# One stage's attention values, token mixing and u, woven two pieces of the channel mixing later

## The chip, the cores and the metric

The kernel runs on one core of a Trainium2 chip. The metric is the time of one execution on the device in microseconds (us); lower is better. A profile of one execution goes with it, which records when each engine ran each instruction. The engines are TensorE (PE in the profile, with its weight loads as PEld), VectorE (DVE), ScalarE (ACT), GpSimd (POOL) and SyncE (SP, which issues DMAs).

## What is computed

Eight batches of attention over pooled keys and values, followed by a token-mixing and a channel-mixing layer with a residual. Cut to what matters:

```python
# q, k, v: (8 batches, 8 heads, 576 tokens, 64); pool = 8
k_p = k.reshape(B, H, Sp, pool, D).mean(axis=3)
v_p = v.reshape(B, H, Sp, pool, D).mean(axis=3)
scores = scale * np.matmul(q, k_p.transpose(0, 1, 3, 2))
attn = softmax(scores)
x = np.matmul(attn, v_p)            # heads side by side: (8, 576, 512)

xt = x.transpose(0, 2, 1)
h = np.maximum(xt @ w_tok1, 0.0) @ w_tok2       # over the tokens
u = x + h.transpose(0, 2, 1)
h2 = np.maximum(u @ w_ch1, 0.0) @ w_ch2         # over the channels, 1536 wide
out = u + h2
```

## The kernel before

The batches are numbered from 0, so "the fourth batch" is batch 3. Of a batch's 576 tokens, 512 form its main part, as four interleaved sets of 128 (j = 0 to 3); the last 64 are its tail. Tails are joined in pairs, batches (0, 7), (1, 2), (3, 4) and (5, 6), so that a pair fills 128 partitions. Work on a pair's tail happens with one of its two batches.

The steps of a batch, with the lines that appear in the profile:

- Loads of k, q and v on GpSimd's DMA queue (L138, L142, L146), started by `load_gated`: a small copy (L984) on GpSimd waits until the last transposed weights of an earlier batch are there, and the loads, a pairing of k (L269) and the pooling of v by additions (L357 to L359) stand behind it on that engine.
- q is turned by a DMA on the SP queue (L693), k is pooled by matmuls (L282 or L291), the scores are a matmul (L390), VectorE subtracts the maximum (L396, L398), ScalarE takes the exponential (L406).
- The weights are turned by a DMA transpose on the SP queue (L412, for a tail L535) into pT. There are two of them for each of the units a (j = 0, 1) and c (j = 2, 3).
- The values, `do_AV`: pT is the stationary operand and pooled v the moving one (L468). VectorE divides by the sum (L472, L473) and writes x. A `do_AV` is called a value block here.
- Token mixing: `do_tails` (L608) and, in two halves, `do_AT` (L615); the first half is activated by ScalarE (L591) and the second by VectorE (L593). Then u for each j (`do_u`, L672 with the addition L673 on VectorE), which a DMA transpose on SP turns, two j at a time (`do_uT`, L684, into uTm).
- Channel mixing, `c_stream`: twelve `do_GT` of four matmuls over 512 columns (L1007, activated by ScalarE in L1009), then for each j three thirds of an output block (L1023, four matmuls each), an addition on VectorE (L1027) and a store on the SP queue (L1055). For the second batch of a pair the same follows for the tail. Each `do_GT` and each third carries the cost 864 and is called a piece here.

The order of instructions on every engine is the order in which the program emits them; no scheduler moves them. A loop over the batches b emits, in each turn, a main stream and a side stream. The main stream is the channel mixing of batch b. The side stream holds what comes next: the turn of q for batch b+2, the gated loads for batch b+3, the value blocks, token mixing and u of batch b+1 (`value_stream`, `mix_stream`), and the scores of batch b+2 (`score_stream`). Each step has a cost in units, and `weave` merges the two streams: it takes a side step when the side's share of its cost is not ahead of the main stream's share. The main stream's count starts at minus `delay`, so that this much of it goes ahead of the first side step, and `lead` takes that much off its length, so that the side stream ends earlier:

```python
tm, ts = max(main.total() - delay - lead, 1e-9), max(side.total(), 1e-9)
cm, cs = -delay, 0.0
...
take_side = im >= len(main.items) or (ia < len(side.items) and cs / ts <= cm / tm)
```

PSUM tiles come from six rotating buffers, pT tiles from six, uTm and q's turned tiles from two each. A step's DMAs are issued where the step is emitted, and a queue takes its DMAs in order.

Of the kernel before, what the change touches and what calls it, by code (L numbers as in the profile page):

```python
# [28 lines left out]
def weave(main, side, delay=0.0, lead=0.0):  # L29


    tm, ts = max(main.total() - delay - lead, 1e-9), max(side.total(), 1e-9)
    im = ia = 0
    cm, cs = -delay, 0.0
    while im < len(main.items) or ia < len(side.items):
        take_side = im >= len(main.items) or (ia < len(side.items) and cs / ts <= cm / tm)
        if take_side:
            c, fn = side.items[ia]
            ia += 1
            cs += c  # L40
        else:
            c, fn = main.items[im]
            im += 1
            cm += c
        fn()
# [3 lines left out]
def kernel(  # L49
# [17 lines left out]
    B, H, S, D = q.shape  # L67
# [864 lines left out]
    def score_stream(st, b):  # L932

        add = adder(st)
        a, c, t = parts[b]
        own = owned(b)
        add(SC, a.do_S, 0)
        add(SC, a.do_S, 1)
        add(0, a.do_E, 0)
        for bb in own[1:]:  # L940
            add(KP, pool_k, bb)
        add(SC, a.do_S, 2)
        add(0, a.do_E, 1)
        add(0, a.do_E, 2)
        add(0, a.do_PT, 0)
        add(0, a.do_PT, 1)
        if t:
            add(2 * SC, t.do_S)
        add(SC, c.do_S, 0)
        if t:  # L950
            add(0, t.do_E)
            add(0, t.do_PT)
        add(SC, c.do_S, 1)
        add(0, c.do_E, 0)
        add(SC, c.do_S, 2)
        add(0, c.do_E, 1)
        add(0, c.do_E, 2)
        add(0, c.do_PT, 0)
        add(0, c.do_PT, 1)

    def value_stream(st, b):

        add = adder(st)
        a, c, t = parts[b]
        if b + 1 < B:
            units(b + 1)
            add(0, qT_dma, b + 1)
        if b + 2 < B:
            add(0, load_gated, b + 2, lambda: c.pT[1][:, 0, 0:1])
        add(AV, a.do_AV, 0)  # L970
        add(AV, a.do_AV, 1)
        if t and len(t.bs) == 1:
            add(AV, t.do_AV)
        add(AV, c.do_AV, 0)
        if t and len(t.bs) > 1:
            add(AV, t.do_AV)
        add(AV, c.do_AV, 1)
        mix_stream(st, b, owned(b + 1)[:1] if b + 1 < B else ())
# [70 lines left out]
    def c_stream(b):  # L1049
        st = Stream()  # L1050
        g = group_of[b]

        def dst_main(j, cols, o_sb):
            q = nc.gpsimd if b == B - 2 and j == 0 else nc.sync if cols.start == 0 else nc.scalar
            q.dma_start(out=out[b, 0:MAIN, cols].rearrange("(p j) n -> p j n", j=NJ)[:, j, :], in_=o_sb)  # L1055

        def dst_tail(j, cols, o_sb):
            for s, bb in enumerate(groups[g]):
                nc.sync.dma_start(out=out[bb, MAIN:S, :], in_=o_sb[half[s], :])

        wide, chunk = channel_mix(lambda kk, t0, t1: uT_main[b][:, t0 // P:t1 // P, kk, :],
                                  lambda j: u_main[b][:, j, :], dst_main, MAIN, 0 if b else 3)
        blocks = [wide] + [chunk(j, 2 if b == B - 1 and j == NJ - 1 else 1) for j in range(NJ)]
        if slot_of[b] == 1:
            wide, chunk = channel_mix(lambda kk, t0, t1: uT_tail[g][:, kk, t0:t1], lambda j: u_tail[g], dst_tail, P)
            at = 3 if b == B - 1 else len(blocks)
            blocks[at:at] = [wide, chunk(0)]
        for block in blocks:
            st.items.extend(block)
        return st  # L1070
# [16 lines left out]
    with tc.manual_schedule(engines=engines):  # L1087
        side1 = begin()
        for b in range(B):
            side = Stream() if b else side1  # L1090
            if 0 < b < B - 1:
                value_stream(side, b + 1)
            if b + 2 < B:
                score_stream(side, b + 2)

            weave(c_stream(b), side, 1728.0 if b == 0 else 3456.0 if b == 1 else 1728.0, 3456.0 if b == B - 2 else 1728.0)


# [28 lines left out]
```

## Time and profile before

| | us |
|---|---|
| median of three runs | 281.32 |
| lowest and highest | 279.86, 281.5 |
| the profiled execution | 280.83 |
| its span, first to last instruction | 279.1 |

The granted clock of TensorE was 1.0 of full speed. In the lines below a row of a timeline has its start in us, its length in us, the engine, the line, and what it writes and reads; in brackets stands the idle time of the engine before it and who ended it. A row of the chain of waits has a start, a length and what the time went to. A list of waits gives the engine, line and tile, whom it waited for, the sum in us, the number of times and the longest. A row of the windows gives for a stretch its length, the busy time of PE, PEld, DVE, ACT and POOL, the granted clock, the DMA engines' share and GB/s. The stage of interest is the channel mixing of batch 2, from about 95 to 128 us.

### The profile page before, as it was taken

The numbers are of one execution on the slowest core, as the hardware profiler recorded it, in microseconds if no ns is written. First come the engines' busy times: TensorE is split into PE (matmuls) and PEld (weight loads), VectorE is DVE, ScalarE is ACT, GpSimd is POOL, SyncE is SP. The second block draws the span as 40 slices with busy tenths as digits, with TensorE's granted clock in tenths as the row PEclk, the third lists the DMA queues.
The fourth block names the chain that finished last, engine by engine and source line by source line (L and its number), as shares of the span: only waits on it lengthen the run. The fifth ranks groups of instructions, "written<-read, shape, count | busy, mean of one in ns | idle before, by whom it ended". The sixth has DMA issues, their size and how long they took to land.

```text
span 279.1 us, 5476 instructions
## 1 busy us (share of the span) xinstructions
PE 268.3 (96%) x2144; PEld 145.1 (52%) x2172; DVE 165.6 (59%) x381; ACT 121.9 (44%) x225; POOL 113.4 (41%) x162
## 2 busy tenths in 40 slices
PE   6789999999999999999999999999999999999994
PEld 4565856554545444475545454475544454554462
DVE  5597677778759853684579761785479452510112
ACT  8673688235533454035534452054623550036220
POOL 8748433697538957193449264820000000000000
PEclk9999999999999999999999999999999999999999
DMA  8999999996999999959998999759266701461013
GB/s 134 176 195 205 200 205 196 190 212 140 197 153 193 222 239 153 212 151 155 173 197 144 204 199 194 162 137 162 63 84 152 180 2 39 113 100 33 38 47 105
DMA packets 98969, 42.27 MB, mean 151 GB/s; under 512 B 68800, under 2 KB 94400, under 8 KB 98944
## 3 DMA queue, kind: packets, MB, share of 16 engines
q0 software_dynamic: 35616, 17.93, 49.1%
q1 hardware_dynamic: 63184, 23.93, 42.4%
q8 instruction: 17, 0.28, 0.4%
q10 hardware_dynamic: 144, 0.07, 0.1%
q14 instruction: 8, 0.07, 0.1%
HBM read 35.85 MB, written 9.44 MB: 162 GB/s over the span
## 4 chain that ended last, share of the span: by engine, by line
PE 84%; DMA 6%; DVE 5%; issue 1%; ACT 1%; POOL 1%; DVEq 0%; POOLq 0%
PE pa L1023 31%; PE pa L1007 30%; PE pa L672 3%; DMA pT<-prob_m 3%; PE pa L390 3%; PE pa L468 3%; DMA km<-in_k_dram 2%; PE pa L597 2%; PE pa L651 1%; DVE xm L473 1%; PE pa L615 1%; PE pt L615 1%; DVE mx L396 1%; PE pa L1039 1%; PE pt L374 1%
## 5 line engine op out<-in xcount | busy, mean ns | idle before, releaser
L1023 PE MATMUL pa<-wc,GT 128*128 128x512 bf16 (+2 forms) x427 | 102.4, 373 | 1.0 <-issue 0.2
L1009 ACT ACTIVATE GT<-pa 128x512 bf16<-128x512 f32 x105 | 62.2, 597 | 64.1 <-PE pa L1007 63.8
L1007 PE MATMUL pa<-uTm,wc 128*128 128x512 bf16 x372 | 89.3, 379 | 0.0
L1007 PEld LDWEIGHTS <-wc 128*128 128x128 bf16 x564 | 44.8, 98 | 37.1 <-issue 1.6
L1023 PEld LDWEIGHTS <-GT 128*128 128x128 bf16 x444 | 40.8, 98 | 41.5 <-issue 1.2
L406 ACT ACTIVATE prob_m<-sh 128x432 bf16<-128x432 f32 (+1 forms) x48 | 24.5, 522 | 55.2 <-DVE sh L398 55.1
L1027 DVE TENSOR_TENSOR o<-pa,um 128x512 f32<-128x512 f32 (+2 forms) x33 | 22.1, 670 | 26.4 <-PE pa L1023 26.3
L357 POOL TENSOR_TENSOR s<-vs 72x512 f32<-72x512 bf16 x24 | 27.6, 1150 | 15.7 <-DMA vs<-in_v_dram 14.2
L398 DVE TENSOR_TENSOR sh<-pa,mx 128x432 f32<-128x432 f32 (+1 forms) x48 | 26.8, 558 | 4.1
L396 DVE TENSOR_REDUCE mx<-pa 128x6 f32<-128x432 f32 (+1 forms) x48 | 26.4, 550 | 4.3 <-PE pa L390 4.1
L473 DVE TENSOR_TENSOR xm<-pa,den 128x256 bf16<-128x256 f32 x56 | 23.7, 424 | 1.9
L1055 POOL DMA_DIRECT2D out_dram<-o x1 | 0.6, 620 | 49.1 <-DVE o L1027 49.1
L472 DVE RECIPROCAL den<-pa 128x4 f32<-128x4 f32 x60 | 10.6, 176 | 16.8 <-PE pa L468 16.7
L673 DVE TENSOR_TENSOR um<-pa,xm 128x512 bf16<-128x512 f32 x24 | 16.1, 687 | 5.0 <-PE pa L672 3.7
L358 POOL TENSOR_TENSOR s<-s 72x256 f32<-72x256 f32 x24 | 17.3, 722 | 1.9
L390 PE MATMUL pa<-kbd,qT 128*128 128x144 bf16 x128 | 15.2, 226 | 0.9 <-ACT qT L378 0.7
L390 PEld LDWEIGHTS <-qT 128*128 128x128 bf16 x128 | 10.6, 98 | 9.3 <-ACT qT L378 1.3
L468 PEld LDWEIGHTS <-pT 72*128 72x128 bf16 (+1 forms) x256 | 11.2, 99 | 8.1 <-DMA pT<-prob_m 1.4
L593 DVE TENSOR_SCALAR AT<-pa 128x512 bf16<-128x512 f32 x6 | 4.1, 692 | 16.9 <-PE pa L615 9.5
L672 PE MATMUL pa<-AT,w2m 128*128 128x512 bf16 x45 | 13.1, 379 | 0.0
L468 PE MATMUL pa<-vpx,pT 72*128 72x65 bf16 (+1 forms) x256 | 12.6, 194 | 0.5 <-DMA pT<-prob_m 0.4
L1007 PE MATMUL pa<-uTt,wc 128*128 128x128 bf16 x192 | 11.9, 219 | 0.0
(151 smaller groups left out, 273.5 us busy)
## 6 DMA issues: line engine op xcount, KB each, us to landing
out_dram<-o SPq DMA_DIRECT2D x30, 256.0 KB, 2.6
vs<-in_v_dram POOLq DMA_DIRECT2D x7, 512.0 KB, 10.7
km<-in_k_dram POOLq DMA_DIRECT2D x7, 512.0 KB, 9.6
qm<-in_q_dram POOLq DMA_DIRECT2D x7, 512.0 KB, 12.8
wc<-in_moe_w_ch_dram POOLq DMA_DIRECT2D x6, 512.0 KB, 11.7
out_dram<-o SPq DMA_DIRECT2D x8, 128.0 KB, 2.4
o<-in_k_dram SPq DMA_DIRECT2D x2, 256.0 KB, 3.0
kt<-in_k_dram POOLq DMA_DIRECT2D x8, 64.0 KB, 8.0
```

Source lines behind the costliest of these rows:

```text
L357: nc.gpsimd.tensor_tensor(out=s4, in0=vs[:, hs, 0:4], in1=vs[:, hs, 4:8], op=add)
L390: nc.tensor.matmul(out=sc[:, (h - h0) * 2:(h - h0) * 2 + 2, :], lhsT=qTs[self.b][:, 2 * h + self.jj, :], rhs=kbd[self.b % NB][:, h], start ...
L396: nc.vector.tensor_reduce(out=mx[:, 0:n], in_=sc, axis=AX.X, op=ALU.max)
L398: nc.vector.tensor_tensor(out=sh[:, 0:n], in0=sc, in1=mx[:, 0:n, None].broadcast_to([P, n, SP]), op=ALU.subtract)
L406: nc.scalar.activation(out=self.probs[:, :, h0:h1, 0:SP].rearrange("p e h n -> p h e n"), in_=self.sh[i][:, 0:(h1 - h0) * 2].rearrange("p ...
L468: nc.tensor.matmul(out=ao[r, hh, :], lhsT=probs_of(h, r), rhs=vpx[b % NB][:, h, :], start=True, stop=True)
L473: nc.vector.tensor_tensor(out=xo[rows, hf * HP * D:(hf + 1) * HP * D].rearrange("p (h d) -> p h d", d=D), in0=ao[rows, :, 0:D], in1=den[ro ...
L672: nc.tensor.matmul(out=u_ps, lhsT=w2m[:, m, j, :], rhs=ATs[b][:, m, :], start=(m == 0), stop=(m == 1))
L1007: nc.tensor.matmul(out=g_ps[:, i, :], lhsT=wc1[:, kk, m * P:(m + 1) * P], rhs=uTs(kk, 0, width), start=(kk == 0), stop=(kk == 3))
L1009: nc.scalar.activation(out=GT[:, m0:m0 + per, :], in_=g_ps, func=AF.Relu)
L1023: nc.tensor.matmul(out=hold["ps"], lhsT=GT[:, kk, j * P:(j + 1) * P], rhs=wc2[:, kk, cols], start=(kk == 0), stop=(kk == NM - 1))
L1027: nc.vector.tensor_tensor(out=o_sb, in0=hold["ps"], in1=us(j)[:, cols], op=ALU.add)
```

## The change

One argument, the delay, in the loop over the batches. It was 1,728 units in the first turn, 3,456 in the turn of batch 1, and 1,728 afterwards. Now the turn of batch 2 has 3,456 as well. Nothing else is edited.

```diff
-            weave(c_stream(b), side, 1728.0 if b == 0 else 3456.0 if b == 1 else 1728.0, 3456.0 if b == B - 2 else 1728.0)
+            weave(c_stream(b), side, 1728.0 if b == 0 else 3456.0 if b <= 2 else 1728.0, 3456.0 if b == B - 2 else 1728.0)
```

In the turn of batch 2 the emitted order is, before and now (GT0 to GT11 and out0.0 to out3.2 are pieces, a and c the value blocks, t that of the tail pair, S the scores of batch 4, tGT and outT the tail's channel mixing):

```
before: GT0-1 | a.AV0 | GT2-3 | a.AV1 | GT4-5 | c.AV0 | GT6-7 | t.AV | GT8 | c.AV1 | GT9-10 | tails | GT11
        | AT.0 | out0.0 | AT.1 | out0.1-2 | u0 | out1.0 | u1 | out1.1 | uT0, u2 | out1.2 | u3 | out2.0
        | uT2, a.S0 | out2.1 | a.S1 | out2.2, out3.0 | a.S2 | out3.1-2 | c.S0 | tGT0 | c.S1 | tGT4-8 | c.S2 | outT
now:    GT0-3 | a.AV0 | GT4-5 | a.AV1 | GT6-7 | c.AV0 | GT8 | t.AV | GT9-10 | c.AV1 | GT11, out0.0 | tails
        | AT.0 | out0.1-2 | AT.1 | out1.0 | u0 | out1.1 | u1 | out1.2 | uT0, u2 | out2.0 | u3 | out2.1
        | uT2, a.S0 | out2.2 | a.S1 | out3.0-1 | a.S2 | out3.2 | c.S0 | tGT0-4 | c.S1 | tGT8 | c.S2 | outT
```

The turn of q for batch 4 and the gated loads of batch 5 are emitted just ahead of a.AV0 in both.

## The prediction

> **What bounds the kernel now.** I read the page first, then the waits, then the chain of waits in order of time around the fourth batch, then the timelines of the engines there. Batches are numbered from 0, so the fourth batch is batch 3. Its values, token mixing and u are woven into the channel mixing of batch 2.
>
> ```profile
> span 279.1 us, 5476 instructions
> PE 268.3 (96%) x2144; PEld 145.1 (52%) x2172; DVE 165.6 (59%) x381; ACT 121.9 (44%) x225; POOL 113.4 (41%) x162
> ```
>
> TensorE (PE) is busy in 96% of the span, and no other engine in more than 59%. A change of order that issues the same matmuls can therefore only gain the stretches in which PE stands, or make new ones. So the first question is which waits of PE the profile names in the place that the change touches.
>
> ```profile
> PEld L468 <- DMA pT<-prob_m: 1.4, 2, 0.9
> ...
> PE pa L468 <- DMA pT<-prob_m: 0.4, 1, 0.4
> ```
>
> In these lists of waits L468 is the matmul of the values, attention weights times pooled v. Its stationary operand is pT, the transposed weights, which a DMA on the SP queue writes. The weight loader waited for that DMA twice, 1.4 us in sum, and the matmul itself once for 0.4 us. The chain of waits says when.
>
> ```profile
> 91.01 6.13 DMA pT<-prob_m
> 97.15 0.04 issue
> 97.19 0.43 PE pa L468 x8
> 97.63 0.56 PE pa L1007 x3
> 98.18 3.21 DMA pT<-prob_m
> 101.39 0.05 issue
> 101.44 0.43 PE pa L468 x8
> ```
>
> Two of batch 3's transposes reach PE at the last moment: the first, issued at 91.01, lands at 97.14 and the matmuls begin at 97.19; the third, issued at 98.18, lands at 101.39 and its matmuls begin at 101.44. What PE does around them stands in its timeline:
>
> ```profile
> 94.94 1.89 PE L1007 MATMUL pa<-uTm,wc 128*128 128x512 bf16 x8
> 97.19 0.43 PE L468 MATMUL pa<-vpx,pT 72*128 72x65 bf16 x8 [0.36 <-DMA pT<-prob_m]
> 97.46 1.89 PE L1007 MATMUL pa<-uTm,wc 128*128 128x512 bf16 x8
> 99.19 0.42 PE L468 MATMUL pa<-vpx,pT 72*128 72x65 bf16 x8
> 99.45 1.89 PE L1007 MATMUL pa<-uTm,wc 128*128 128x512 bf16 x8
> 101.44 0.43 PE L468 MATMUL pa<-vpx,pT 72*128 72x65 bf16 x8
> 101.71 1.89 PE L1007 MATMUL pa<-uTm,wc 128*128 128x512 bf16 x8
> ```
>
> Each L1007 row holds two pieces of the channel mixing, four matmuls of 512 columns each. Where nothing waits, two pieces take 97.46 to 99.19, which is 1.73 us or 0.865 us a piece (0.216 us a matmul), and a value block takes 0.26 to 0.27 us (99.19 to 99.45). Against this spacing the first pair lasts from 94.94 to 97.19, 2.25 us, and so holds a wait of 0.52; the third lasts from 99.45 to 101.44, 1.99 us, a wait of 0.26. Together 0.78 us.
>
> **The change part by part.** In the weave the channel mixing starts from a negative count. With a delay of 1,728 units two pieces of 864 go ahead of the first side step; with 3,456 units four do. The side stream of this stage has 17,198 units, and the main stream 25,920, of which 25,920 - 1,728 - 1,728 = 22,464 were spread over before and 20,736 are now. So the side steps start two pieces later, run closer together and have caught up at the end. In the built order the value blocks come two pieces later, or nearly, token mixing, u and the scores of batch 4 about one piece later, and from the tail's channel mixing on one score block alone differs. Matmuls are neither added nor removed. The order on ScalarE is the same, and on GpSimd only buffer names differ.
>
> *The waits that go.* The first value block will begin at 94.94 + 4 x 0.865 = 98.40, with pT there since 97.14: 1.26 us to spare. The third block comes after eight pieces and two blocks, at 94.94 + 6.92 + 0.53 = 102.39, with its pT there since 101.39: 1.0 us to spare. When pT lands doesn't hang on the move, since the four transposes are issued between 91 and 101 from work that stands ahead of it. Both waits go: **minus 0.78 us**. From below this is bounded by the idle time that the windows show,
>
> ```profile
> 96.00:98.00 2.00, 1.64 (x15) 0.76 (x14) 1.34 (x4) 1.42 (x3) 1.84 (x3) 1.00 1.19 301
> ...
> 100.00:102.00 2.00, 1.90 (x17) 0.83 (x15) 0.86 (x5) 1.19 (x2) 0.00 (x0) 1.00 1.07 194
> ```
>
> where PE (second figure) lacks 0.36 and 0.10 us, 0.46 in sum, at a granted clock of 1.00; from above by the loader's 1.4 us. I take 0.78, since it is a distance between starts.
>
> The Trainium skill, "Perfetto Trace Analysis", section "Per-instruction lifecycle: what the profiler-reported window actually captures", says that the end of a TensorE instruction is estimated by the profiler and only the start is observed. By the modelled ends the gain would be 0.46 us, by the starts 0.78; the trace bears the page out, as the L1007 row of 1.89 us from 97.46 overlaps the value block that starts 1.73 us later.
>
> Another page speaks against the cover: "TensorE: Matmul & The Clock Gate" of the Trainium skill, section "Back-to-back issue gap", gives about 131 ns per matmul of 512 columns in a sustained stream. By that the four pieces would end at 94.94 + 16 x 0.131 = 97.04, 0.1 us before pT lands, and a little of the first wait would stay. The trace has 0.216 us, and goes.
>
> *Token mixing to u.* Before, two pieces stand between the second half of token mixing (L615) and u (L672); now one does, and VectorE has the first output block's addition (L1027) to do ahead of the activation instead of after it.
>
> ```profile
> 110.01 1.03 PE L615 MATMUL pa<-xm,w1m 128*128 128x512 bf16 x4
> 110.87 1.89 PE L1023 MATMUL pa<-wc,GT 128*128 128x512 bf16 x8
> 112.60 0.59 PE L672 MATMUL pa<-AT,w2m 128*128 128x512 bf16 x2
> ```
>
> ```profile
> 111.07 0.69 DVE L593 TENSOR_SCALAR AT<-pa 128x512 bf16<-128x512 f32 x1 [4.77 <-PE pa L615]
> ...
> 112.80 0.69 DVE L1027 TENSOR_TENSOR o<-pa,um 128x512 f32<-128x512 f32 x1 [1.03 <-PE pa L1023]
> ```
>
> Put in these times: the piece after token mixing starts at 110.87 and u at 110.87 + 0.865 = 111.74; u's first matmul reads the half that ScalarE wrote, the second, at 111.95, the half that VectorE finishes at 111.76. So 0.2 us to spare. The addition of 0.69 us becomes possible a token-mixing half (0.86 us) earlier and is over before. Cost: nothing; 0.5 us if the addition starts so late that all of its 0.69 us lies ahead of the activation.
>
> *SP's queue and batch 4.* Each side step takes its DMA along. qT of batch 4 keeps its place. The first turn of u goes behind the second output store, and the two turns follow each other; scores of batch 4 come one piece later, so the last ones' reduction on VectorE now stands ahead of the last output addition.
>
> ```profile
> 115.25 1.23 SPq L684 DMA_TRANSPOSE uTm<-um  x1
> 117.40 0.33 SPq L1055 DMA_DIRECT2D out_dram<-o  x1
> 118.00 1.28 SPq L684 DMA_TRANSPOSE uTm<-um  x1
> 121.34 2.51 SPq L1055 DMA_DIRECT2D out_dram<-o  x2
> 123.95 6.86 SPq L412 DMA_TRANSPOSE pT<-prob_m  x4
> ```
>
> The next rows are from the timelines of VectorE and PE; the last two are the landings of batch 4's pT and, over 84 to 140 us, of the turns of u.
>
> ```profile
> 121.78 0.46 DVE L398 TENSOR_TENSOR sh<-pa,mx 128x288 f32<-128x288 f32 x1
> ...
> 128.37 1.89 PE L1007 MATMUL pa<-uTm,wc 128*128 128x512 bf16 x8
> 130.09 0.42 PE L468 MATMUL pa<-vpx,pT 72*128 72x65 bf16 x8
> ...
> 134.33 0.42 PE L468 MATMUL pa<-vpx,pT 72*128 72x65 bf16 x8
> ...
> DMA to landing us min/median/max: 3.3/3.3/4.7
> ...
> DMA to landing us min/median/max: 3.0/4.0/9.5
> ```
>
> The second turn will be issued near 118 as now and is first read by the channel mixing of batch 3, which now starts at 128.37 - 0.78 = 127.6. Even after 9.5 us, the longest landing of a turn, it is there at 127.5. Nothing is added. Batch 4's four pT are issued back to back for 6.86 us, so a delay of the first is one of all: the last goes out near 123.95 + 6.86 - 1.3 = 129.5, lands 3.3 us later, at 132.8, and is read at 134.33. That is 1.5 us to spare. The last scores' reduction and subtraction (0.46 us in the row, and about as much for the reduction) now stand ahead of the last addition, and delay it, the last store and the transposes behind it by about 0.25 us against PE. Cost: nothing.
>
> *GpSimd.* Its order stays, and its next load waits for the fourth pT of batch 3, which doesn't move:
>
> ```profile
> 102.78 0.19 POOL L984 COPY gate<-pT 128x1 bf16<-128x1 bf16 x1 [3.14 <-DMA pT<-prob_m]
> ...
> 118.18 1.14 POOL L357 TENSOR_TENSOR s<-vs 72x512 f32<-72x512 bf16 x1 [5.74 <-DMA vs<-in_v_dram]
> ```
>
> The loads of batch 5 begin at 102.9 in both kernels, and PE wants nothing of them before the channel mixing of batch 3. Cost: nothing. Nor do PSUM's six rotating buffers bind: two are held through token mixing of batch 3, as before, and the others come free after a VectorE or ScalarE pass of 0.7 us or less (two for scores), four or more steps before they are wanted.
>
> The sum is -0.78 us. The profiled execution took 280.83 us (1.7 us around its span), so it would take 280.05. The three runs lie from 279.86 to 281.5 with the median at 281.32, 0.5 above the profiled one; the mean of the four is 280.88, which gives **280.1 us**.
>
> **The rivals.** *The gain is lost again later.* The loads of batch 5 keep their time while PE comes 0.78 us earlier, so that a wait could grow where PE meets them. Against it speaks that PE's list of waits names no other DMA that it waits for after the start of the kernel. The time: 280.8.
>
> *Batch 4's transposes come late.* The wait taken from batch 3 returns one stage on. Four pT stand in one row on SP behind two stores, and what PE has to spare at the last of them is 1.5 us. Should they land as slowly as batch 3's first, after 6.1 us instead of 3.3, they would be 2.8 + 0.25 late, a wait of 1.55 us, and the sum is 1.55 - 0.78 = 0.77 above now: 281.6. It decides from a delay of 1.5 us on, and is slower than now from 2.3. Against it: the run of four showed 4.7 us at most, and the loads of batch 5 have landed by 118.18, when GpSimd starts on the last of them.
>
> *The change doesn't remove the wait*, because PE waits for something else that becomes ready with pT. The values are the only other operand, and GpSimd ended its pass over them before these transposes were issued; the starts follow the landings by 0.05 us twice. It would give 280.8 as well, and goes with the first rival.
>
> **How the numbers follow.** The forecast gets 0.68, no gain 0.17, the late transposes 0.12; 0.03 is left for what I don't see. The range takes the upper bound of the gain, 280.83 - 1.4 = 279.4, the slower rival's 281.6, and some of the spread of the runs on both sides: 279.0 to 281.8. A per cent is 2.8 us, about what a measurement of this kernel can tell from no change; no case reaches it by itself. So within 1%: 0.89. Slower by more gets 0.07, for the slower rival where two batches pay it or the landing is that of 9.5 us; faster by more 0.04.
>
> **What would show it.** Right: in the new profile L468 no longer waits for pT, the four pieces from about 94.9 run at 0.86 us each, the first value block starts near 98.4 and the third near 102.4, and the channel mixing of batch 3 starts near 127.6 instead of 128.37. The AT step shows no PE wait ahead of L672. Wrong: an idle time of PE ahead of L672 near 112 us or of L468 near 130 to 134 us, or a start of batch 3's channel mixing at 128.3 or later.

## The result and the profile after

| | before | changed |
|---|---|---|
| median, 20 runs each (us) | 281.17 | 280.06 |
| lowest and highest | 279.61, 282.25 | 279.35, 281.59 |
| span of the profiled execution | 279.1 | 278.6 |

The ratio of the times is 0.9963 with a 95% interval of 0.9947 to 0.9978. On 281.17 us that is a gain of 1.04 us, between 0.62 and 1.49. The ratios in this document leave out runs more than 1.5% above the fastest run of the same kernel, which were one of `fill_after`'s twelve and four of `q_late`'s six.

First the page of the changed kernel, then PE's timeline around batch 3's values and at the end of the stage:

```profile
span 278.6 us, 5477 instructions
PE 267.4 (96%) x2144; PEld 145.0 (52%) x2172; DVE 165.8 (60%) x381; ACT 121.8 (44%) x225; POOL 113.8 (41%) x162
```

```profile
95.17 3.62 PE L1007 MATMUL pa<-uTm,wc 128*128 128x512 bf16 x16
98.63 0.42 PE L468 MATMUL pa<-vpx,pT 72*128 72x65 bf16 x8
98.89 1.89 PE L1007 MATMUL pa<-uTm,wc 128*128 128x512 bf16 x8
100.61 0.42 PE L468 MATMUL pa<-vpx,pT 72*128 72x65 bf16 x8
100.88 1.89 PE L1007 MATMUL pa<-uTm,wc 128*128 128x512 bf16 x8
102.70 0.43 PE L468 MATMUL pa<-vpx,pT 72*128 72x65 bf16 x8
...
111.26 1.03 PE L615 MATMUL pa<-xm,w1m 128*128 128x512 bf16 x4
112.13 1.03 PE L1023 MATMUL pa<-wc,GT 128*128 128x512 bf16 x4
112.99 0.59 PE L672 MATMUL pa<-AT,w2m 128*128 128x512 bf16 x2
...
127.89 1.89 PE L1007 MATMUL pa<-uTm,wc 128*128 128x512 bf16 x8
129.62 0.42 PE L468 MATMUL pa<-vpx,pT 72*128 72x65 bf16 x8
```

The first four pieces run from 95.17 to 98.63, 3.46 us or 0.865 us each: no wait. The two pieces ahead of the third value block take 100.88 to 102.70, 1.82 us, which leaves a wait of 0.09. Token mixing, one piece and u follow each other in steps of 0.87 and 0.86 us: the removed piece wasn't needed as cover. From the first piece of batch 2's channel mixing to the first piece of batch 3's, "the stage" from here on, it is 32.72 us, against 33.43 before (94.94 to 128.37): 0.71 us less.

The idle time by modelled ends shows less of it. These are the windows over the stage, before and after; the second figure is PE's:

```profile
94.90:128.00 33.10, 32.48 (x237) 16.83 (x239) 19.74 (x45) 13.14 (x24) 21.25 (x29) 1.00 1.13 186
```

```profile
94.90:128.00 33.10, 32.94 (x241) 17.25 (x242) 19.88 (x46) 13.11 (x24) 21.33 (x29) 1.00 1.17 200
```

In these 33.1 us PE lacked 0.62 us before and lacks 0.16 now, 0.46 less, while the stage by its starts is 0.71 us shorter. The distance between starts is what the kernel gains.

The whole span fell by 0.5 us only, since this execution reached the stage 0.23 us later (95.17 for 94.94). PE's list of waits of the changed kernel has L468 no more, and a wait at the start of the kernel that the first profile of before didn't have:

```profile
PE pt L494 <- DMA qt<-in_q_dram: 1.1, 1, 1.1
```

### The profile page after: what moved, and what is told of

Its sections match the earlier page's. It is cut to its first block, busy times and chain, and to the rows that moved or that the text cites. A ratio compares the mean times of both kernels' runs of the same rounds, so it can differ in the third digit from the quotient of the medians.

```text
span 278.6 us, 5477 instructions
## 1 busy us (share of the span) xinstructions
PE 267.4 (96%) x2144; PEld 145.0 (52%) x2172; DVE 165.8 (60%) x381; ACT 121.8 (44%) x225; POOL 113.8 (41%) x162
## 4 chain that ended last, share of the span: by engine, by line
PE 88%; DVE 4%; DMA 3%; POOL 2%; issue 1%; ACT 1%; POOLq 0%; DVEq 0%
PE pa L1023 33%; PE pa L1007 31%; PE pa L672 3%; PE pa L390 3%; DMA qt<-in_q_dram 3%; PE pa L468 3%; PE pa L597 2%; PE pa L651 1%; PE pa L615 1%; DVE xm L473 1%; PE pt L615 1%; PE pa L1039 1%; PE pa L677 1%; PE pa L635 1%; PE pa L282 1%
## 5 line engine op out<-in xcount | busy, mean ns | idle before, releaser
L1009 ACT ACTIVATE GT<-pa 128x512 bf16<-128x512 f32 x105 | 62.1, 597 | 61.9 <-PE pa L1007 61.6
L1007 PE MATMUL pa<-uTm,wc 128*128 128x512 bf16 x372 | 89.1, 379 | 0.0
L1007 PEld LDWEIGHTS <-wc 128*128 128x128 bf16 x564 | 45.0, 98 | 36.7 <-issue 0.8
L468 PEld LDWEIGHTS <-pT 72*128 72x128 bf16 (+1 forms) x256 | 11.3, 99 | 7.3 <-issue 0.8
L468 PE MATMUL pa<-vpx,pT 72*128 72x65 bf16 (+1 forms) x256 | 12.6, 194 | 0.0
L269 POOL COPY kk<-km 128x1024 bf16<-128x1024 bf16 x8 | 8.1, 1036 | 9.6 <-DMA km<-in_k_dram 6.7
L1007 PE MATMUL pa<-uTt,wc 128*128 128x128 bf16 x192 | 11.9, 219 | 0.0
```

The lines of the kernel that those rows point to most:

```text
L468: nc.tensor.matmul(out=ao[r, hh, :], lhsT=probs_of(h, r), rhs=vpx[b % NB][:, h, :], start=True, stop=True)
L1007: nc.tensor.matmul(out=g_ps[:, i, :], lhsT=wc1[:, kk, m * P:(m + 1) * P], rhs=uTs(kk, 0, width), start=(kk == 0), stop=(kk == 3))
L1009: nc.scalar.activation(out=GT[:, m0:m0 + per, :], in_=g_ps, func=AF.Relu)
```

## The experiments

Every reading below is a distance between starts in PE's timeline. Lag 1 is the start of the first value block after the start of the pieces ahead of it, less 0.865 us for each piece; lag 3 the same for the third value block.

| kernel | stage from, to | stage | lag 1 | lag 3 | stage less lags |
|---|---|---|---|---|---|
| before | 94.94, 128.37 | 33.43 | 0.52 | 0.26 | 32.65 |
| before, second profile | 95.18, 129.84 | 34.66 | 1.72 | 0.30 | 32.64 |
| rest_only | 95.11, 129.20 | 34.09 | 1.08 | 0.36 | 32.65 |
| later_stages | 94.73, 129.27 | 34.54 | 1.53 | 0.36 | 32.65 |
| changed | 95.17, 127.89 | 32.72 | 0 | 0.09 | 32.63 |
| values_only | 95.18, 127.92 | 32.74 | 0 | 0.12 | 32.62 |
| delay_one | 94.56, 127.46 | 32.90 | 0 | 0.27 | 32.63 |
| delay_six | 94.89, 127.51 | 32.62 | 0 | 0 | 32.62 |
| all_stages | 94.50, 127.12 | 32.62 | 0 | 0 | 32.62 |

The last column is the result of this study: whatever is moved, the stage takes 32.62 to 32.65 us plus what PE waits for batch 3's pT. A stage that has the same steps and no such wait agrees: batch 4's takes 32.62 us in the first profile of before (156.80 to 189.42).

**Which of the moved parts brings it.** `values_only` puts only the value blocks later, `rest_only` only what stands behind them. Each replaces the weave of batch 2 by a list that says how many pieces stand ahead of each side step:

```diff
+            if b == 2:
+                main, at = c_stream(b).items, 0
+                for (_, step), n in zip(side.items, AHEAD):
+                    for _, piece in main[at:n]:
+                        piece()
+                    at = n
+                    step()
+                for _, piece in main[at:]:
+                    piece()
+                continue
```

> Only the five value blocks of batch 3 come two pieces later; tails, token mixing, u and the scores of batch 4 stand where they stood before. Theory (the gain is PE's two waits for pT of batch 3): the stage from the first piece of batch 2's channel mixing to the first piece of batch 3's takes 32.7 us, as with the whole change (32.72), against 33.43 before, and the time is 0.7 us or more below before. Rival (the gain comes from the later order of token mixing, u, scores and their DMAs): the stage stays near 33.4 us and the time as before.

> The complement: the value blocks stand where they stood before, and tails, token mixing, u and the scores of batch 4 stand as in the changed kernel. Theory: no gain, PE waits for pT ahead of the first and third value block as before, stage near 33.4 us. Rival: the gain of the changed kernel, stage near 32.7 us.

Measured: `values_only` 0.9966 (0.9943 to 0.9989) of before, `rest_only` 1.0007 (0.9986 to 1.0028). PE's timeline of `rest_only`:

```profile
95.11 1.89 PE L1007 MATMUL pa<-uTm,wc 128*128 128x512 bf16 x8
97.92 0.43 PE L468 MATMUL pa<-vpx,pT 72*128 72x65 bf16 x8 [0.92 <-DMA pT<-prob_m]
98.19 1.89 PE L1007 MATMUL pa<-uTm,wc 128*128 128x512 bf16 x8
99.92 0.42 PE L468 MATMUL pa<-vpx,pT 72*128 72x65 bf16 x8
100.18 1.89 PE L1007 MATMUL pa<-uTm,wc 128*128 128x512 bf16 x8
102.27 0.43 PE L468 MATMUL pa<-vpx,pT 72*128 72x65 bf16 x8 [0.21 <-DMA pT<-prob_m]
```

Both waits stand there still, and larger than in the first profile of before, so its stage took 34.09 us and not the 33.4 expected. The value blocks bring the gain; the later token mixing, u and scores neither add to it nor cost anything, as far as 0.2% in the times and 0.03 us in the last column can tell.

**Is PE really idle there.** `fill_before` and `fill_after` put four idle matmuls ahead of the first value block, in the order of before and in the changed one:

```diff
+                side.items.insert(2, (0, lambda: warm(4)))
```

> The order of before with four idle matmuls of 512 columns (0.86 us of PE, their result unused) put ahead of the first value block of batch 3. Theory: they fit into the waits (0.52 us there, 0.26 at the third block), so the stage grows by 0.1 us at most, to about 33.5, and the time stays as before. Rival (PE doesn't stand there, the profile's gaps are only modelled): the stage grows by 0.86 us to 34.3 and the time by 0.3%.

> The changed kernel with the same four idle matmuls ahead of the first value block. Theory: nothing is left to hide them, the stage grows from 32.72 by 0.86 us to 33.6, about that of fill_before, and the gain of the change is gone. Rival: the two orders take the idle matmuls alike, fill_after stays about 0.7 us below fill_before.

Measured: `fill_before` 1.0000 (0.9978 to 1.0022), `fill_after` 0.9984 (0.9961 to 1.0007); stages 33.88 (94.95 to 128.83) and 33.48 us (94.82 to 128.30). In `fill_before` the idle matmuls (L261) take the place of the first wait:

```profile
94.95 1.89 PE L1007 MATMUL pa<-uTm,wc 128*128 128x512 bf16 x8
96.68 1.03 PE L261 MATMUL pa<-idle 128*128 128x512 bf16 x4
97.58 0.43 PE L468 MATMUL pa<-vpx,pT 72*128 72x65 bf16 x8
...
101.90 0.43 PE L468 MATMUL pa<-vpx,pT 72*128 72x65 bf16 x8 [0.17 <-DMA pT<-prob_m]
```

The 0.86 us of extra work cost the order of before nothing that the times show; the rival's 0.3% lies outside the interval. In the changed order the stage grew by 0.76 us, from 32.72 to 33.48: 0.86 for the matmuls, less the 0.09 that PE waited there. The expectation for the stage of `fill_before`, 33.5, missed by 0.4 us: the third pT landed later than in the first profile, and 0.33 us of lag 3 stayed. Between the two kernels the times decide nothing: `fill_after` was expected level with `fill_before`, or 0.7 us below it by the rival, and its ratio is 0.16% or 0.4 us below, with intervals that overlap. The traces have the same 0.4 us, and it is what was left of the waits in `fill_before` (0.04 and 0.33): less these and the 0.86 us, the two stages are 32.65 and 32.62, as in the table.

**How much delay it takes, and where.** One piece more than before (`delay_one`), four more than before (`delay_six`), the longer delay in other turns instead (`later_stages`), and in all of them (`all_stages`):

```diff
-  3456.0 if b == 1 else 1728.0
+  3456.0 if b == 1 else 2592.0 if b == 2 else 1728.0       # delay_one
+  3456.0 if b == 1 else 5184.0 if b == 2 else 1728.0       # delay_six
+  3456.0 if b <= 1 or 3 <= b <= 5 else 1728.0              # later_stages
+  3456.0 if 1 <= b <= 5 else 1728.0                        # all_stages
```

> Batch 2's delay is 2,592 units, one piece more than before and one less than in the changed kernel. Theory (PE waits for pT of batch 3, which lands at its own time): in the five profiles so far the third pT lands 0.8 to 1.4 us after PE would want it in the order of before, so one piece (0.865 us) covers most of that: waits of 0 to 0.6 us stay, the stage takes 32.7 to 33.3 us. Rival (the two pieces matter for what they put late, not for the cover): half the gain, with no wait for pT left or all of it.

> Batch 2's delay is 5,184 units, two pieces more than in the changed kernel. Theory: nothing is left to cover, so no further gain: stage 32.7 us, time as the changed kernel's, unless the later scores of batch 4 make PE wait for batch 4's pT, whose spare time shrinks by what they come later. Rival (later is better by itself, because the side steps run in a denser row): a further gain of about 0.5 us.

> The delay of batch 2 as before; those of batches 3, 4 and 5 get the 3,456 units instead. Theory: PE waits for no pT there, so no gain, time as before within 0.1%, and in the profile PE's waits for pT of batch 3 are still there. Rival (a longer delay helps any stage): 0.3% for each stage, about 1% in all.

> The changed kernel with 3,456 units also in the turns of batches 3, 4 and 5. Theory: PE waits for no pT in those, so nothing beyond the changed kernel: ratio to before 0.996, stage of batch 2 32.7 us. Rival (from the 0.2% that the later stages alone may have given): ratio 0.994.

Measured: `delay_one` 0.9964 (0.9947 to 0.9982), `delay_six` 0.9954 (0.9932 to 0.9975), `later_stages` 0.9980 (0.9956 to 1.0004), `all_stages` 0.9984 (0.9956 to 1.0013). One piece more covers the first wait and leaves 0.27 us of the third; four more cover all, and batch 4's transposes still come in time. `later_stages` kept the waits for batch 3's pT (1.4 and 0.2 us by the modelled ends), and the longer delay did nothing where it was put: the stages of batches 3, 4 and 5 take 28.43, 32.62 and 27.80 us in the first profile of before and in `later_stages` alike. So the delay isn't good by itself. The 0.2% of `later_stages`, where at most 0.1% was expected, is not clear of none. Nor is the 0.2% of `all_stages`, where 0.4% was expected; its stage has no wait, and one of its twelve runs took 283.5 us. The medians of `delay_six`, 279.78 us, and `all_stages`, 279.80, are below the changed kernel's 280.06, but they were taken at other times, and all the intervals overlap. Whether one of the two beats the change stays open; the trace leaves 0.09 us to be had.

**How far the waits vary.** The kernel before was profiled a second time.

> The kernel before, unchanged, for a second profile of it. Theory (the gain in time, 1.0 us, is above the 0.71 us seen between the two profiled stages because the first profile of before caught early landings): the third pT of batch 3 lands later than in the first profile, PE's lag at the third value block is 1.0 to 1.9 us instead of 0.78, and the stage takes 33.7 to 34.5 us. Rival (the rest of the gain comes from elsewhere): the stage takes 33.4 us again. The ratio of times is 1.000 and shows what the interval is worth.

```profile
95.18 1.89 PE L1007 MATMUL pa<-uTm,wc 128*128 128x512 bf16 x8
98.63 0.43 PE L468 MATMUL pa<-vpx,pT 72*128 72x65 bf16 x8 [1.56 <-DMA pT<-prob_m]
98.90 1.89 PE L1007 MATMUL pa<-uTm,wc 128*128 128x512 bf16 x8
100.62 0.42 PE L468 MATMUL pa<-vpx,pT 72*128 72x65 bf16 x8
100.89 1.89 PE L1007 MATMUL pa<-uTm,wc 128*128 128x512 bf16 x8
102.92 0.43 PE L468 MATMUL pa<-vpx,pT 72*128 72x65 bf16 x8
```

The time was 1.0013 of before (0.9991 to 1.0034), and its two waits 1.72 and 0.30 us, 2.02 in sum, against 0.78 in the first profile. That and the stage, 34.66 us, lie a little above the ranges expected (where "lag at the third value block" means this sum). The third wait carries no bracket in this profile although the pieces ahead of it took 2.03 us instead of 1.73: the modelled ends hide it. Four profiles with the value blocks where they were before have 0.78, 1.44, 1.89 and 2.02 us. The first was the smallest, but none of the four is a typical execution: the first took 0.34 us less than the median of its kernel, the other three 0.32, 1.02 and 1.23 us more. If the executions of a kernel differed in these waits alone, which is not shown, the median execution would wait 0.8 to 1.1 us; this estimate fits the gain of 1.04 us.

**Why the pT land late.** `q_late` and `q_mid` keep the order of before in the weave and issue batch 4's load of q later on GpSimd: after all sums of its v, or after half of them.

```diff
-        load(b, (0, 2, 1) if slot_of[b] else (0, 1, 2))
+        load(b, (0, 2) if b == 4 else (0, 2, 1) if slot_of[b] else (0, 1, 2))
         if b == 4:
             sum_v(3, 2, H)
+            sum_v(4, 0, 4)               # q_mid only
+            load(4, (1,))                # q_mid; in q_late behind the last sum_v(b)
         else:
             pair_k(b)
-        sum_v(b)
+        sum_v(b, 4 if b == 4 else 0)     # q_mid only
```

> The order of before in the weave; batch 4's load of q (512 KB) is issued after GpSimd's sums of its v, near 100 us, instead of near 76, so that the loads in flight end earlier. It tells where the late landing comes from. Theory A (the transposes of batch 3 queue behind transfers that batch 4's loads hold up): batch 3's first pT pair lands in 3 to 4.5 us instead of 6 to 7, PE's waits for pT are gone or below 0.3 us in sum, the stage takes about 32.8 us in the order of before, and the time is 0.2 to 0.4% below before. Theory B (the transposes are slow by themselves when two follow a store): the landings stay at 6 us and more, the stage at 33.4 us or more.

> The order of before in the weave; batch 4's load of q is issued after half of the sums of its v, near 95 us, instead of near 76 (before) or 100 (q_late). Theory: the first pT pair of batch 3 lands in 3 to 4 us, so the first wait is gone; the later pair, issued near 97, now shares the DMA engines with that load and may land a little late; PE's lag at the third value block is 0 to 0.5 us, and q's turn is done well before the scores near 118, so q_late's 6 us wait is gone. Time 0.2 to 0.4% below before, as with the change. Rival (any later load of q costs more than the wait): time above before.

Measured: both are slower than before, `q_late` 1.0125 (1.0064 to 1.0185), `q_mid` 1.0122 (1.0096 to 1.0149). The ratio of `q_late` rests on two runs, 282.63 and 286.32 us; the median of all six, 287.46 against 281.26, is 2.2% above before. So `q_mid`'s rival, that a later load costs more than the wait, is what happened. But the two answer the question. These rows give the landing of batch 3's four pT (least, median, longest, in us after the issue) in the second profile of before, in `q_late` and in `q_mid`:

```profile
DMA to landing us min/median/max: 3.2/4.1/7.2
```

```profile
DMA to landing us min/median/max: 3.1/3.2/3.3
```

```profile
DMA to landing us min/median/max: 3.1/4.1/8.7
```

Without q's 512 KB on its way all four land in 3.1 to 3.3 us, and both waits are gone in the order of before (the edit adds lines, so L1007 is L1008 here and L1009 in `q_mid`):

```profile
95.00 1.89 PE L1008 MATMUL pa<-uTm,wc 128*128 128x512 bf16 x8
96.72 0.42 PE L468 MATMUL pa<-vpx,pT 72*128 72x65 bf16 x8
...
98.97 1.89 PE L1008 MATMUL pa<-uTm,wc 128*128 128x512 bf16 x8
100.70 0.42 PE L468 MATMUL pa<-vpx,pT 72*128 72x65 bf16 x8
```

In `q_mid` the load goes out at 93.66, and now it is the second pair, issued at 96.70, that lands after up to 8.7 us, a wait of 4.89 us by the starts in place of 0.30:

```profile
98.80 1.89 PE L1009 MATMUL pa<-uTm,wc 128*128 128x512 bf16 x8
105.42 0.48 PE L468 MATMUL pa<-vpx,pT 72*128 72x65 bf16 x8 [4.74 <-DMA pT<-prob_m]
```

So the transposes are late where q's load is in flight; in this theory A holds, though the stage and the time that it forecast did not come. The first pair of `q_mid`, issued before the load went out, landed after 3.1 to 3.3 us too.

The two waits come about differently, as SP's rows show, first those of the second profile of before, then those of `q_late`:

```profile
91.34 6.16 SPq L412 DMA_TRANSPOSE pT<-prob_m  x2
...
99.62 2.67 SPq L412 DMA_TRANSPOSE pT<-prob_m  x2
```

```profile
91.07 2.66 SPq L412 DMA_TRANSPOSE pT<-prob_m  x2
...
96.88 2.63 SPq L412 DMA_TRANSPOSE pT<-prob_m  x2
```

The first pT landed 7.2 us after its issue. The third landed within 3.3 us of its own; it came late because SP issued it at 99.62 instead of 96.88, after 6.16 us with the first pair. The two turns of u (uTm and uTt) that stand ahead of the pT on SP's queue were slow as well: 10.4 and 8.3 us to landing, against 5.2 and 4.2 in `q_late`. That a load in flight holds up a transpose itself is shown by `q_mid`: the tail's pT, issued at 94.50 behind transposes that landed after 3.1 to 3.3 us, took 10.0 us, about until q's load was there (issued at 93.66, 10.7 us). How much of the late landings in the order of before came this way, and how much through the slow turns ahead, these runs don't separate.

The Trainium skill, "DMA: Bandwidth & Descriptors", section "Queues, rings and completion order", says that each DMA engine takes turns between the queues that have work for it. The longer landings beside the load agree with that, but no run here shows the turns.

My expectations of the time missed: that of `q_mid` took the sharing to cost half a microsecond, and that of `q_late` overlooked that q's own turn waits for its load. That turn was issued at 107.42, while batch 5's loads were in flight, and took 15.7 us to land. The scores of batch 4 stood 6.0 us for it (shown at the end).

## Why the prediction was right

The time, 280.06 us for 280.1, and the mechanism hold; the single steps:

- *PE bounds the kernel, and its waits for pT are all that the move can win.* Shown: the stage less these waits is the same within 0.03 us in nine profiles.
- *Minus 0.78 us for the two waits.* Right in kind; measured 0.71 between the profiled stages, and 1.04 (0.62 to 1.49) in the times. The term was taken from one execution, and three more profiles of that order have 1.44 to 2.02. That the first profile caught early landings is the likely reason why the times gained more than the sum; the interval holds 0.78 as well. That the time was met within 0.04 us is luck: the 280.88 that I started from is 0.29 below the median of the twenty runs, 281.17, and the gain was 0.26 too small.
- *Starts, not modelled ends, give the size* (0.78 against 0.46). Shown twice: the stage fell by 0.71 where PE's idle time fell by 0.46, and the constant last column comes out of starts alone.
- *1.26 and 1.0 us to spare.* Too much, for the same reason as the sum: in the changed kernel's own profile the first pT landed 0.35 us ahead of its block (issued at 91.38, 6.9 us to landing, block at 98.63), and the third block waits 0.09 us. By the second profile of before, whose third pT arrives 102.92 - 95.18 = 7.74 us into the stage, where the changed order wants it at 102.39 - 94.94 = 7.45, a wait of 0.3 us would stay.
- *Token mixing to u, SP's queue, batch 4, PSUM: nothing.* Right. `rest_only` measured these together: no difference in time, and 32.65 us less the waits. One reading was wrong without harm: 9.5 us is the longest landing of a turn of u from 84 us on, but the turn issued at 82.3 us took 10.7, and with that the second turn would have been late. In the changed kernel the two turns landed after 3.6 and 3.2 us.
- *GpSimd's loads don't move.* Its order doesn't, but they began at 104.1 us in the profile of the changed kernel and not at 102.9, because the fourth pT, for which they wait, landed later there. That is the variation of the landings, not the change: the second profile of before has 104.4.
- *The rivals.* Batch 4's transposes came in time even with four pieces more than before. The gain was not lost later: PE's list of waits after the change has nothing new behind the start.

## What to carry to other kernels

Where an engine that bounds the kernel waits for a transfer, put work that is already there between issue and use; here it cost nothing, as the moved steps had time of their own, and moving only the waiting steps was enough. Size such a wait by the distance between starts, and from several profiles: what a transfer takes under other traffic varied here by more than the wait in one profile. Moving the traffic instead was the worse cure here, as it had a date of its own to keep.

## What the runs showed of the hardware

A long wait costs more than its length. In `q_late` PE stood 6.0 us for q's turn; the windows give the granted clock (third figure from the end):

```profile
112.00:117.00 5.00, 5.00 (x25) 1.00 1.53 156
117.00:120.00 3.00, 0.20 (x1) 1.00 1.34 170
120.00:123.20 3.20, 0.00 (x0) 0.55 1.23 175
123.20:125.00 1.80, 1.80 (x6) 0.50 1.19 325
125.00:127.00 2.00, 1.78 (x8) 0.50 0.08 15
127.00:129.00 2.00, 2.00 (x12) 0.96 0.01 2
```

The clock was halved after some 3 us of idleness (117.2 to 120.3), and it stayed so for about 4 us of work after the wait, which is about 2 us more. The stage adds up with that: 40.72 us (95.00 to 135.72) are 32.6, the 6.2 that PE stood by the starts, and 2. In `q_mid` the wait of 4.9 us ended with the clock still at 1.00; it was halved at about 105.65, 5.0 us after the matmuls before the wait, for some 3.4 us of work. Its stage of 39.20 us adds up as 32.6, 4.9 and 1.7.

The Trainium skill, "TensorE: Matmul & The Clock Gate", Part 1 on the clock gate, gives at least one idle window of about 3.4 us as the point. The 5.0 us agree, and the 3.1 us fall a little short of it. The waits that the change removes, 1.7 us at most, left the clock at 1.00.
